# The third transform step one piece later, and the component sum of z ahead of its split

## The chip, the cores and the metric

One core of one Trainium2 chip runs the whole kernel. The time is that of the device for one execution, in microseconds; 2408.49 us is the median of three runs before the change (2408.03 to 2408.72). Shorter is better.

## The reference

For x of shape 2 x 1 x 4096 x 640 the kernel computes a gated mix of a spectral mixer a and a feed-forward block b:

```python
Xf = rfft2(x, axes=(1, 2))                    # 4096 tokens -> 2049 frequencies
zr, zi = Xf.real, Xf.imag                     # 4 blocks of 160 channels
hr = relu(zr @ w1[0] - zi @ w1[1] + b1[0])
hi = relu(zi @ w1[0] + zr @ w1[1] + b1[1])
or_ = hr @ w2[0] - hi @ w2[1] + b2[0]
oi_ = hi @ w2[0] + hr @ w2[1] + b2[1]
or_, oi_ = shrink(or_, 0.01), shrink(oi_, 0.01)
a = irfft2(or_ + 1j * oi_)
b = (gelu(x @ w_gate) * (x @ w_up)) @ w_down  # 640 -> 1728 -> 640
out = g * a + (1 - g) * b                     # g = sigmoid(sum(x * gate_w))
```

All values are 32-bit floats.

## The kernel before, in words

TensorE multiplies in a rounded format (float32r), so the kernel splits each operand into a high part (a rounded copy, helper `high`, L290, on ScalarE) and a low part (what the rounding left, helper `low`, L293, mostly a VectorE subtraction that reads the high part). A product is then the sum of two or three matmuls. PSUM has 8 banks, which `bank()` hands out in turn; each holds one result until the other engines have emptied it. The schedule is manual: each engine runs its instructions in the order in which the code issues them, and the waits between engines follow from which tiles and banks they share.

The work has three stages.

1. **Feed-forward up, with the first transform between its pieces** (to about 1278 us). There are 39 pieces: 3 groups of feature tiles x 13 pieces of tokens. The first piece runs `plain`, every other one `quad` for each of its four or five tiles; each quad has 7 places (`hook(0)` to `hook(6)`) where other work is issued. In pieces 14 to 24 and 26 to 36 these places also carry the first transform: 64 steps, one for each of two batches and 32 token residues. The list `steps_a` says which piece i, and which of its slots j, takes step k. A step loads x (`a_load`, SP's queue), splits it twice (`a_split`), computes a part of the gate (`a_gate`, L819) and runs two halves `a_step` (L832: two matmuls each, with L833 and L834 emptying the banks), and a store of the result (scr, SP's queue). Both halves multiply with tables `f`, one tile for each half with a single buffer; each set of tables serves four steps in a row, and `f1_load` (L797, on GpSimd's queue) fetches the next set behind the step k with k % 4 == 1.

2. **The spectral layers** (about 1278 to 1715 us). 16 chunks of frequencies x 4 blocks of channels are 64 steps. In step i the program issues: every fourth time, `rest` for the next chunk (a transform without sums, tile zz); `main_z` for step i + 1; `mlp1` for step i; `mlp2` for step i - 1; and every second step `y_split` and `inv1` for a pair of earlier blocks. `main_z` calls `fwd2`: eight matmuls (L1001) put the real and imaginary components of z side by side in one bank `pz`. The z copy (ScalarE, L290) and the z subtraction (VectorE, L293) split both components; the zt copy (ScalarE, L1013) takes the imaginary one and the addition (VectorE, L1016) makes zt = real + imaginary of it. `mlp1` multiplies the split zs of such a sum (tiles sh, sl) first, into a bank that ScalarE copies as kc (L1104); then VectorE forms hs from two more results and kc (L1111). Between the two, `sums()` splits zt of the next step into zs. ScalarE then rounds relu(hs) to h (L1064), VectorE subtracts (L1065), and a last bank is emptied by ScalarE (L1117) and VectorE (L1118). `mlp2` ends in m (L1148) and y (L1149). `y_split` makes ys; `inv1` ends in copies `is` on ScalarE (L1184) and VectorE (L1186).

3. **Inverse transform and feed-forward down** (from about 1715 us): 32 steps of `down`, which add both into the output.

The list and the four instructions that the change touches are

```python
    steps_a = [(i, j) for i in (*range(14, 25), *range(26, 37))
               for j in ((0, 1, 2) if i in (15, 17, 22) else (0, 1) if i < 26 or i == 36 else (3,) if i == 26 else (0, 1, 2, 3))]
```

and the body of `fwd2`, below with the functions that call it.

Of the kernel before, what the change touches and what calls it, by code (L numbers as in the profile page):

```python
# [234 lines left out]
def spectral_mix_kernel(ctx: ExitStack, tc: tile.TileContext, a):  # L235
    nc = tc.nc
# [11 lines left out]
    def bank():  # L248
        return psum.tile([P, 512], F32, name="bank", tag="bank")
# [39 lines left out]
    def high(dst, src, scale=1.0):  # L289
        nc.scalar.activation(dst, src, AF.Copy, scale=scale)  # L290

    def low(dst, src, hi, eng=nc.vector):
        eng.tensor_sub(dst, src, hi.bitcast(F32))  # L293

    def split(dst_h, dst_l, src, eng=nc.vector):

        high(dst_h, src)
        low(dst_l, src, dst_h, eng)
# [658 lines left out]
    def part_of(b, c, k):  # L957

        if not wide(b, c):
            return tiny([P, CH], name=("zt", "kc", "hs")[k])  # L960
        if not WT:
            WT.append(mid([P, 3, CW], name="wt"))
        return WT[0][:, k]
# [32 lines left out]
    def fwd2(b, c, o, z, zs=None):  # L996

        pz = bank()
        for kp in range(4):
            ft = F2[0 if c == 0 and kp == 0 else 1]  # L1000
            nc.tensor.matmul(pz.rearrange("p (r e k f) -> p k r e f", r=2, e=2, k=4)[:, kp], SC[b, c, kp][:, o:o + P],  # L1001
                             ft.rearrange("p (r e f) -> p r e f", r=2, e=2), start=True, stop=True)
        F = width(b, c)
        if F > CH:
            zz = [z[h][:, :, :F].rearrange("p r (e n) -> p r e n", e=2)[..., :P] for h in range(2)]
            pr = pz.rearrange("p (r e n) -> p r e n", r=2, e=2)
        else:
            zz, pr = [z[h][:, :, :F] for h in range(2)], pz.rearrange("p (r n) -> p r n", r=2)
        high(zz[0], pr)
        if zs:  # L1010
            t = part_of(b, c, 0)
            t4 = t[:, :F].rearrange("p (e n) -> p e n", e=2)[..., :P] if F > CH else t[:, :F]
            nc.scalar.activation(t4, pr[:, 1], AF.Copy)  # L1013
        low(zz[1], pr, zz[0])
        if zs:
            nc.vector.tensor_add(t4, pr[:, 0], t4)  # L1016
        if wide(b, c):
            pn = bank()
            for q in range(2):
                nc.tensor.matmul(pn[:, :4], SC[q, c, 0][:, o:o + P], fny[:, 4 * q:4 * q + 4], start=q == 0, stop=q == 1)  # L1020
            split(*(z[h][:, :, :F].rearrange("p r (e n) -> p r e n", e=2)[..., P] for h in range(2)),
                  pn[:, :4].rearrange("p (r f) -> p r f", r=2))
            if zs:
                nc.vector.tensor_copy(t[:, :F].rearrange("p (e n) -> p e n", e=2)[..., P], pn[:, :2])
        return lambda: split(zs[0][:, :F], zs[1][:, :F], t[:, :F])

    def rest(b, c):

        z = zmid(b, c, [P, 2, 2, width(b, c)], F32R, name="zz")
        fwd2(b, c, 4 * P, [z[:, h] for h in range(2)])  # L1030
        d = zld[b][c]
        if wide(b, c):
            st(d, z.rearrange("p h r f -> p (h r f)").bitcast(F32))
        else:
            st(dr(d, 0, [[4 * CW, P], [CW, 4], [1, CH]]), z[:, :, :, :CH].rearrange("p h r f -> p (h r) f").bitcast(F32))
# [12 lines left out]
    def main_z(b, c, n):  # L1048
        F = width(b, c)
        z = two(b, c, "z")  # L1050
        if wide(b, c):
            zs = small([P, 2, F], F32R, name="zs")
            zs = [zs[:, h] for h in range(2)]
        else:
            if chunks.index((b, c)) < 2 * NCH - 4:
                zs = mid([P, 2, F], F32R, name="zs")
                zs = [zs[:, h] for h in range(2)]
            else:
                zs = [tiny([P, F], F32R, name="zs") for h in range(2)]
        Z[b, c, n] = z, zs  # L1060
        return fwd2(b, c, P * n, z, zs)
# [472 lines left out]
    def spread(i, s, fs):  # L1534

        for k, f in enumerate(fs):
            j, q = i, max(s + k, 0)
            while j < last and q >= points(j):
                j, q = j + 1, q - points(j)
            slots.setdefault((j, q), []).append(f)  # L1540
    steps_a = [(i, j) for i in (*range(14, 25), *range(26, 37))
               for j in ((0, 1, 2) if i in (15, 17, 22) else (0, 1) if i < 26 or i == 36 else (3,) if i == 26 else (0, 1, 2, 3))]

    def back(i, s, f):
        if s < 0:
# [2 lines left out]
    for k, (b, n2) in enumerate(a_seq):  # L1548
        i, j = steps_a[k]
# [42 lines left out]
    for j in range(7):  # L1592
        p0, p1, p2 = wd_pre(j)
        i = 2 * KEYS
# [190 lines left out]
```

## Time and profile before

| what | value |
|---|---|
| median of three runs | 2408.49 us |
| the profiled execution | 2407.91 us, span 2406.1 us |
| granted TensorE clock | 1.000 |
| TensorE busy | 2397.7 us (100%) |
| VectorE busy | 1969.7 us (82%) |
| ScalarE busy | 1464.5 us (61%) |
| GpSimd busy | 143.0 us (6%) |
| DMA | 503.08 MB, mean 209 GB/s |

By stage, with the busy time of each engine (us):

| stretch | TensorE | VectorE | ScalarE |
|---|---|---|---|
| 0 to 1278 (1278) | 1275.20 | 992.34 | 752.94 |
| 1278 to 1715 (437) | 436.45 | 374.24 | 346.46 |
| 1715 to 2406 (691) | 686.01 | 603.15 | 365.14 |

In rows of the profile PE is TensorE, PEld its loading of weights, DVE VectorE, ACT ScalarE, POOL GpSimd and SP the engine that issues most DMAs. In rows in order of time the columns are start (us from the start of the span), duration (us), engine, line, operation, result<-operands, shapes and number; brackets hold how long the engine was idle just before, and what ended that. In rows of waits the numbers are us in total, how many times, and the longest. In rows by stretch each engine has its busy time and its number of instructions, in the order PE, PEld, DVE, ACT, POOL; then come the granted clock, the DMA share and GB/s.

### The profile page before, as it was taken

What the parts mean: (1) busy time and instruction counts of PE and PEld (TensorE: products, weight loads), DVE (VectorE), ACT (ScalarE), POOL (GpSimd) and SP (SyncE); (2) the same over time, 40 slices, a digit from 0 to 9 for tenths busy, and PEclk for the clock granted to TensorE, in tenths of its full rate; (3) what the DMA queues carried; (4) which work ended last, traced back from release to release, by engine and by line L of the source; (5) the groups of instructions that cost most, each with busy time, mean ns of one, the idle gap of its engine ahead of it and who ended that gap; (6) DMA issues with size and microseconds to landing.
All of it is one profiled execution on the core that took longest, in us unless ns stands there. A gap on an engine that the chain in (4) does not pass through costs nothing.

```text
span 2406.1 us, 49143 instructions
## 1 busy us (share of the span) xinstructions
PE 2397.7 (100%) x18047; PEld 2391.9 (99%) x18047; DVE 1969.7 (82%) x4150; ACT 1464.5 (61%) x3332; POOL 143.0 (6%) x213
## 2 busy tenths in 40 slices
PE   9999999999999999999999999999999999999999
PEld 9999999999999999999999999999999999999999
DVE  8777779777778888888857888888898888888887
ACT  5544456665566666666645788888755555555554
POOL 0111110000000000000001111111000000000000
PEclk9999999999999999999999999999999999999999
DMA  5666666777776777868766454557955544455543
GB/s 213 246 232 235 229 229 231 257 257 252 254 258 228 242 262 239 287 228 268 250 207 230 130 169 152 163 167 234 339 163 165 165 151 152 145 164 165 163 147 98
DMA packets 319093, 503.08 MB, mean 209 GB/s; under 512 B 24444, under 2 KB 196348, under 8 KB 318852
## 3 DMA queue, kind: packets, MB, share of 16 engines
q1 hardware_dynamic: 298788, 446.65, 55.5%
q0 software_dynamic: 20064, 53.29, 6.2%
q8 instruction: 142, 2.33, 0.4%
q14 instruction: 99, 0.81, 0.1%
HBM read 308.74 MB, written 191.11 MB: 208 GB/s over the span
## 4 chain that ended last, share of the span: by engine, by line
PE 91%; issue 5%; DVE 2%; DMA 1%; ACT 1%; SPq 0%; POOL 0%; POOLq 0%; DVEq 0%; ACTq 0%
PE bank L578 70%; PE bank L312 13%; PE bank L1001 3%; PE bank L709 2%; PE bank L832 1%; DMA f<-in_f_dram 1%; PE bank L1087 1%; PE bank L1088 1%; DMA xraw<-in_xT_dram 0%; DVE w L293 0%; PE bank L1089 0%; DVE xo L293 0%; DVE hs L1111 0%; DVE xd L489 0%; ACT m L1148 0%
## 5 line engine op out<-in xcount | busy, mean ns | idle before, releaser
L578 PE MATMUL bank<-xo,w 128*128 128x320 f32 (+1 forms) x9000 | 1250.4, 297 | 0.7 <-ACT p L605 0.7
L578 PEld LDWEIGHTS bank<-xo,w 128*128 128x128 f32 x9000 | 1220.0, 189 | 1.8 <-ACT p L605 1.1
L578 PE MATMUL bank<-wx,ho 128*128 128x320 f32 x4608 | 631.8, 299 | 1.3 <-DVE ho L293 1.1
L578 PEld LDWEIGHTS bank<-wx,ho 128*128 128x128 f32 x4608 | 627.7, 189 | 1.8 <-DVE ho L293 1.4
L293 DVE TENSOR_TENSOR ho<-hraw,ho 128x640 fp32r<-128x640 f32 (+3 forms) x384 | 194.1, 539 | 24.7 <-ACT ho L290 22.7
L605 ACT ACTIVATE u<-bank 128x320 f32<-128x320 f32 (+1 forms) x250 | 107.4, 430 | 138.1 <-PE bank L578 134.2
L290 ACT ACTIVATE ho<-hraw 128x640 fp32r<-128x640 f32 x320 | 168.9, 571 | 34.5 <-PE bank L578 31.3
L655 DVE TENSOR_TENSOR u<-bank,u 128x320 f32<-128x320 f32 (+1 forms) x165 | 79.9, 485 | 82.7 <-ACT u L605 81.8
L293 DVE TENSOR_TENSOR xs<-xr,xs 64x640 fp32r<-64x640 f32 x128 | 104.9, 820 | 46.6 <-ACT xs L290 43.3
L834 DVE TENSOR_TENSOR as<-bank,as 64x320 f32<-64x320 f32 x256 | 113.8, 483 | 25.9 <-ACT as L833 24.1
L293 DVE TENSOR_TENSOR xo<-xraw,xo 128x640 fp32r<-128x640 f32 (+1 forms) x155 | 125.0, 806 | 8.1 <-ACT xo L290 6.1
L312 PE MATMUL bank<-wm,h 128*128 128x320 f32 (+1 forms) x792 | 129.3, 299 | 0.0
L605 ACT ACTIVATE p<-bank 128x320 f32<-128x320 f32 (+1 forms) x125 | 54.1, 432 | 119.3 <-PE bank L578 61.9
L833 ACT ACTIVATE as<-bank 64x320 f32<-64x320 f32 x256 | 96.6, 426 | 32.3 <-PE bank L832 29.3
L290 ACT ACTIVATE xo<-xraw 128x640 fp32r<-128x640 f32 (+1 forms) x155 | 111.7, 721 | 5.4 <-DMA xraw<-in_xT_dram 3.6
L1405 ACT ACTIVATE bank<-bank 128x320 f32<-128x320 f32 x31 | 13.1, 422 | 166.4 <-PE bank L578 166.4
L312 PEld LDWEIGHTS bank<-wm,h 128*128 128x128 f32 (+1 forms) x792 | 111.8, 186 | 1.1
L1399 DVE SCALAR_TENSOR_TENSOR uu<-bank,gs,uu 128x320 f32<-128x320 f32 x193 | 102.5, 545 | 8.4 <-PE bank L578 4.9
L1371 DVE SCALAR_TENSOR_TENSOR uu<-bank,gs,uu 128x320 f32<-128x320 f32 x120 | 57.9, 545 | 49.2 <-ACT uu L1370 47.1
L290 ACT ACTIVATE xs<-xr 64x640 fp32r<-64x640 f32 x128 | 93.4, 730 | 2.1 <-DMA xr<-in_x_dram 0.3
L606 ACT ACTIVATE h<-bank 128x320 f32<-128x320 f32 (+1 forms) x165 | 71.1, 431 | 35.8 <-PE bank L578 32.8
L605 ACT ACTIVATE pb<-bank 128x320 f32<-128x320 f32 x80 | 35.0, 437 | 88.8 <-PE bank L578 88.6
(184 smaller groups left out, 3520.7 us busy)
## 6 DMA issues: line engine op xcount, KB each, us to landing
xo<-xD SPq DMA_DIRECT2D x96, 640.0 KB
xraw<-in_xT_dram SPq DMA_DIRECT2D x158, 320.0 KB
hD<-h SPq DMA_DIRECT2D x128, 320.0 KB
hraw<-hD SPq DMA_DIRECT2D x128, 320.0 KB
xD<-xo POOLq DMA_DIRECT2D x48, 640.0 KB, 4.4
sc<-scr SPq DMA_DIRECT2D x65, 320.0 KB
xr<-in_x_dram SPq DMA_DIRECT2D x64, 320.0 KB
scr<-as SPq DMA_DIRECT2D x64, 320.0 KB
```

What stands on the lines that cost most here:

```text
L290: nc.scalar.activation(dst, src, AF.Copy, scale=scale)
L293: eng.tensor_sub(dst, src, hi.bitcast(F32))
L312: nc.tensor.matmul(dst, l, by_two(r), start=i == 0, stop=i == len(ops) - 1)
L578: nc.tensor.matmul(dst, l, by_two(r), start=first and i == 0, stop=i == len(ops) - 1, skip_group_check=True)
L605: copy = lambda d, s_: nc.scalar.activation(d, s_, AF.Copy)
L606: gelu = lambda d, s_: nc.scalar.activation(d, s_, AF.Gelu_apprx_tanh)
L655: nc.vector.tensor_add(u4, C, u4)
L833: nc.scalar.activation(stg[hi, cs], pa[lo, :320], AF.Copy)
L834: nc.vector.tensor_add(stg[hi, cs], pa[hi, :320], stg[hi, cs])
L1001: nc.tensor.matmul(pz.rearrange("p (r e k f) -> p k r e f", r=2, e=2, k=4)[:, kp], SC[b, c, kp][:, o:o + P], ft.rearrange("p (r e f) -> p ...
L1371: nc.vector.scalar_tensor_tensor(uu[n2][:, cs], po[:, :320], gs[b][:, k, n2:n2 + 1], uu[n2][:, cs], op0=OP.mult, op1=OP.add)
L1399: nc.vector.scalar_tensor_tensor(dst, x, g, dst, op0=OP.mult, op1=OP.add)
```

## The change

```diff
@@ fwd2 @@
-        high(zz[0], pr)
         if zs:
             t = part_of(b, c, 0)
             t4 = t[:, :F].rearrange("p (e n) -> p e n", e=2)[..., :P] if F > CH else t[:, :F]
             nc.scalar.activation(t4, pr[:, 1], AF.Copy)
+            nc.vector.tensor_add(t4, pr[:, 0], t4)
+        high(zz[0], pr)
         low(zz[1], pr, zz[0])
-        if zs:
-            nc.vector.tensor_add(t4, pr[:, 0], t4)
...
@@ steps_a @@
-               for j in ((0, 1, 2) if i in (15, 17, 22) else (0, 1) if i < 26 or i == 36 else (3,) if i == 26 else (0, 1, 2, 3))]
+               for j in ((0, 1, 2) if i in (15, 18, 22) else (0, 1) if i < 26 or i == 36 else (3,) if i == 26 else (0, 1, 2, 3))]
```

No instruction is added, removed or resized. The second hunk takes the third slot from piece 17 and gives piece 18 one. So step 9 goes from slot 2 of piece 17 to slot 0 of piece 18, step 10 from slot 0 to slot 1 of piece 18, and step 11 from slot 1 to slot 2; all other steps stay. Step 9 is one behind which the next set of tables is loaded.

TensorE, in the first quad of piece 18 (the rows show the first transform's matmuls, L832, which read a table f1, between those of the quad). Before:

```order
L578 MATMUL bank_6594<-xo_6298,w3_4960 128x320 x3
L578 MATMUL bank_6594<-xo_6298,w3_4961 128x320 x3
L832 MATMUL bank_6774<-xs_6731,f1_6686 128x320
L832 MATMUL bank_6778<-xs_6731,f1_6686 128x320
L578 MATMUL bank_6629<-xo_6256,w1_4946 128x320 x6
```

Now:

```order
L578 MATMUL bank_6586<-xo_6298,w3_4960 128x320 x3
L578 MATMUL bank_6586<-xo_6298,w3_4961 128x320 x3
L832 MATMUL bank_6744<-xs_6701,f1_6017 128x320
L832 MATMUL bank_6748<-xs_6701,f1_6017 128x320
L578 MATMUL bank_6620<-xo_6256,w1_4946 128x320 x6
```

f1_6686 is the third set's first half, loaded just before; f1_6017 is the second set's, which three earlier steps have used already. The third set (f1_6760 now) is first read at the next slot, in the fourth quad of the piece.

ScalarE, in a spectral step (z_18147 is the high part of z, zt the sum, kc, zs and h as above; the brackets name the engine or DMA queue whose semaphore an instruction waits for). Before:

```order
L1184 ACTIVATE is_18127<-bank_18128 128x320 [waits DMAHW6_49,PE_49,Activation_49]
L290 ACTIVATE z_18147<-bank_18149 128x512 [waits PE_49]
L1013 ACTIVATE zt_18155<-bank_18149 128x256
L1104 ACTIVATE kc_18164<-bank_18160 128x256 [waits PE_49]
L290 ACTIVATE zs_18148<-zt_18155 128x256 [waits DVE_49]
L1064 ACTIVATE h_18159<-hs_18165 128x512 [waits DVE_49]
```

Now:

```order
L1183 ACTIVATE is_18127<-bank_18128 128x320 [waits DMAHW6_49,PE_49,Activation_49]
L1012 ACTIVATE zt_18154<-bank_18149 128x256 [waits PE_49]
L290 ACTIVATE z_18147<-bank_18149 128x512 [waits DVE_49]
L1103 ACTIVATE kc_18164<-bank_18160 128x256 [waits PE_49]
L290 ACTIVATE zs_18148<-zt_18154 128x256
L1063 ACTIVATE h_18159<-hs_18165 128x512 [waits DVE_49]
```

The zt copy has moved ahead of the z copy; the z copy now waits for VectorE, and the copy to zs no longer does.

VectorE, in the same step. Before:

```order
L1186 COPY is_18127<-bank_18133 128x320 [waits PE_49]
L293 TENSOR_TENSOR z_18147<-bank_18149,z_18147 128x512 [waits PE_49,Activation_49]
L1016 TENSOR_TENSOR zt_18155<-bank_18149,zt_18155 128x256
L1111 TENSOR_TENSOR hs_18165<-bank_18167,kc_18164 128x256 [waits PE_49,Activation_49]
L1111 TENSOR_TENSOR hs_18165<-bank_18167,kc_18164 128x256
```

Now:

```order
L1185 COPY is_18127<-bank_18133 128x320 [waits PE_49]
L1013 TENSOR_TENSOR zt_18154<-bank_18149,zt_18154 128x256 [waits Activation_49]
L293 TENSOR_TENSOR z_18147<-bank_18149,z_18147 128x512 [waits Activation_49]
L1110 TENSOR_TENSOR hs_18165<-bank_18167,kc_18164 128x256 [waits PE_49,Activation_49]
L1110 TENSOR_TENSOR hs_18165<-bank_18167,kc_18164 128x256
```

The addition stands ahead of the subtraction, and each of the two has a wait for ScalarE of its own; before, the one wait of the subtraction served both. Lines behind `fwd2` count one less in the changed kernel.

## The prediction

> **What bounds the kernel now.** I read the page first, then the waits of TensorE, then the waits of the spectral stretch, and last the order of time on three engines inside single steps of it.
>
> ```profile
> PE 2397.7 (100%) x18047; PEld 2391.9 (99%) x18047; DVE 1969.7 (82%) x4150; ACT 1464.5 (61%) x3332; POOL 143.0 (6%) x213
> ```
>
> TensorE is busy for 2397.7 of 2406.1 us, so the kernel can gain 8 us at most without less arithmetic. It can lose more: the other engines only have to make TensorE wait. Its waits that touch the two edits are small:
>
> ```profile
> PE bank L832 <- DMA f<-in_f_dram: 0.9, 1, 0.9
> ...
> PE bank L312 <- DVE hs L1118: 0.5, 2, 0.3
> ```
>
> The first is one wait of the first transform for its weights, the second a pair of waits in the spectral layers. That the spectral layers wait so little does not mean that they have room. These are the waits from 1381 to 1715 us:
>
> ```profile
> ACT zs L290 <- DVE zt L1016: 45.6, 54, 1.0
> ...
> ACT h L1064 <- DVE hs L1111: 12.5, 54, 0.3
> ...
> DVE zz L293 <- ACT zz L290: 3.4, 12, 0.3
> ```
>
> ScalarE waits twice for VectorE in each of 54 steps. Those are links of a ring: h of one step (L1064) to h of the next. I measured the ring from the starts of L1064. Here are four successive ones, with some of what stands between them on ScalarE:
>
> ```profile
> 1399.55 0.63 ACT L1064 ACTIVATE h<-hs 128x512 fp32r<-128x512 f32 x1 [0.24 <-DVE hs L1111]
> ...
> 1403.79 0.58 ACT L290 ACTIVATE z<-bank 128x512 fp32r<-128x512 f32 x1
> ...
> 1406.39 0.63 ACT L1064 ACTIVATE h<-hs 128x512 fp32r<-128x512 f32 x1 [0.25 <-DVE hs L1111]
> ...
> 1409.53 0.59 ACT L290 ACTIVATE z<-bank 128x512 fp32r<-128x512 f32 x1
> 1410.01 0.38 ACT L1013 ACTIVATE zt<-bank 128x256 f32<-128x256 f32 x1
> ...
> 1411.47 0.42 ACT L290 ACTIVATE zs<-zt 128x256 fp32r<-128x256 f32 x1 [0.82 <-DVE zt L1016]
> 1412.14 0.63 ACT L1064 ACTIVATE h<-hs 128x512 fp32r<-128x512 f32 x1 [0.24 <-DVE hs L1111]
> ...
> 1415.90 0.59 ACT L290 ACTIVATE z<-bank 128x512 fp32r<-128x512 f32 x1
> 1416.38 0.38 ACT L1013 ACTIVATE zt<-bank 128x256 f32<-128x256 f32 x1
> ...
> 1418.50 0.63 ACT L1064 ACTIVATE h<-hs 128x512 fp32r<-128x512 f32 x1 [0.18 <-DVE hs L1111]
> ```
>
> The intervals are 6.84, 5.75 and 6.36 us. Call them C (a step that also splits zz), B (one that also copies is) and A (neither); A and C also split ys. The first and the last interval of the regular stretch begin and end here:
>
> ```profile
> 1381.65 0.63 ACT L1064 ACTIVATE h<-hs 128x512 fp32r<-128x512 f32 x1 [0.24 <-DVE hs L1111]
> ```
>
> ```profile
> 1708.67 0.63 ACT L1064 ACTIVATE h<-hs 128x512 fp32r<-128x512 f32 x1 [0.24 <-DVE hs L1111]
> ```
>
> The 54 waits of L1064 give 53 intervals over 327.02 us, B in every second place: 27 B, 12 C (the 12 waits of zz) and 14 A. 27 x 5.75 + 14 x 6.36 + 12 x 6.84 = 326.4 us. So all but 0.6 us of this stretch goes at the ring's own pace, and the ring has no slack against TensorE:
>
> ```profile
> 1382.92 0.47 DVE L1118 SCALAR_TENSOR_TENSOR hs<-bank,b1r,hs 64x256 f32<-64x256 f32 x1
> ```
>
> ```profile
> 1383.45 0.60 PE L312 MATMUL bank<-zs,wm 128*128 128x256 f32 x3 [0.29 <-DVE hs L1118]
> ```
>
> L1118 empties a PSUM bank at 1383.39 and the matmul that takes the bank starts 0.06 us later. Ring and TensorE go side by side, one touching the other. A longer ring lengthens the kernel; a shorter one finds TensorE in the way at once:
>
> ```profile
> 1381.65:1406.34 24.69, 24.35 (x197) 23.97 (x196) 21.43 (x48) 20.22 (x49) 3.13 (x2) 1.00 0.52 160
> ```
>
> This is one chunk of four steps (2B + A + C): 24.69 us, TensorE busy 24.35.
>
> **Edit 1, the third step one piece later.** The step that reads the third set of weights:
>
> ```profile
> 522.93 0.43 PE L832 MATMUL bank<-xs,f 128*128 128x320 f32 x2
> 529.71 0.51 PE L832 MATMUL bank<-xs,f 128*128 128x320 f32 x2 [0.90 <-DMA f<-in_f_dram]
> 533.59 0.43 PE L832 MATMUL bank<-xs,f 128*128 128x320 f32 x2
> 547.44 0.43 PE L832 MATMUL bank<-xs,f 128*128 128x320 f32 x2
> ```
>
> ```profile
> 522.31 0.53 POOL L797 DMA_DIRECT2D f<-in_f_dram  x1 [49.19 <-PE bank L832]
> ```
>
> Each half of the weights has one buffer, so its load is issued only when the last step with the old half is done: here at 522.31, for use some 7 us later, too late by 0.90. With the step in piece 18, old weights serve where 529.71 and 533.59 stand, and the new ones are first read near 547.44: about 18 us from load to use for a transfer that took 7. The wait goes; with the restart of TensorE I take **-1.0 us** (0.9 to 1.1). What else moves with the step: its x load and scr store on SP, two splits, the gate and the evictions. Nothing waits for these two DMAs but the step itself, and pieces 15 and 22 hold a third step already without a row of theirs among TensorE's waits. I cost them at nothing, covered by TensorE's matmuls; if a bank came late there, it would be a part of a microsecond once.
>
> **Edit 2, the addition ahead of the split.** Nothing is added or removed; 64 steps issue the same four instructions on one bank in another order. Before: two copies on ScalarE (z, zt), then a subtraction and the addition on VectorE, one crossing. Now: ScalarE zt, VectorE addition, ScalarE z, VectorE subtraction, three crossings. The rows of the order in the section on the change show that the z copy, which waited for TensorE before, now waits for VectorE. That this is the addition, and not some older work, follows from how such a bank is handled before:
>
> ```profile
> 1415.41 0.82 DVE L293 TENSOR_TENSOR ys<-y,ys 128x640 fp32r<-128x640 f32 x1 [0.20 <-ACT ys L290]
> 1416.79 0.69 DVE L293 TENSOR_TENSOR z<-bank,z 128x512 fp32r<-128x512 f32 x1 [0.55 <-PE bank L312]
> 1417.40 0.41 DVE L1016 TENSOR_TENSOR zt<-bank,zt 128x256 f32<-128x256 f32 x1
> 1417.73 0.74 DVE L1111 TENSOR_TENSOR hs<-bank,kc 128x256 f32<-128x256 f32 x2
> ```
>
> The subtraction needs only the z copy, which ended at 1416.49, and VectorE was free from 1416.23. It started at 1416.79, 0.03 us after the end of the zt copy (1416.76), which only reads the same bank. So on one bank VectorE stands behind everything ScalarE was given ahead of it, and the reverse must hold for the z copy behind the addition. The Trainium skill bears on this (PSUM — Partial Sum Buffer, section on PSUM bank collisions): two engines on one bank at once raise an error, reads against reads too, so programs guard a bank with semaphores. By that rule the wait has to be there and the sum is that of the forecast; by data alone it would be the first rival. The 0.03 us agree with the rule.
>
> Now each interval again, with 0.03 us for a crossing (as above), and with the habit of these rows that an instruction that waits for nothing starts 0.08 us before the end of the one ahead of it on VectorE:
>
> A: zt copy first, 1415.90 + 0.38 = 1416.28; addition 1416.31 to 1416.72; z copy 1416.75 to 1417.34; subtraction 1417.37; 0.61 later (as now) hs at 1417.98 against 1417.73: **+0.25**.
>
> ```profile
> 1409.43 0.89 DVE L1186 COPY is<-bank 128x320 f32<-128x320 f32 x2
> 1410.42 0.69 DVE L293 TENSOR_TENSOR z<-bank,z 128x512 fp32r<-128x512 f32 x1
> 1411.03 0.41 DVE L1016 TENSOR_TENSOR zt<-bank,zt 128x256 f32<-128x256 f32 x1
> 1411.36 0.74 DVE L1111 TENSOR_TENSOR hs<-bank,kc 128x256 f32<-128x256 f32 x2
> ```
>
> B: the zt copy would end at 1409.91, but VectorE copies until 1410.32. Addition 1410.24 to 1410.65; z copy 1410.68 to 1411.27; subtraction 1411.30; hs 1411.91 against 1411.36: **+0.55**. VectorE now stands idle for 0.6 us while ScalarE does what it formerly did during the copies.
>
> ```profile
> 1403.92 0.69 DVE L293 TENSOR_TENSOR zz<-bank,zz 128x512 fp32r<-128x512 f32 x1 [0.28 <-ACT zz L290]
> ...
> 1405.61 0.74 DVE L1111 TENSOR_TENSOR hs<-bank,kc 128x256 f32<-128x256 f32 x2
> ```
>
> C: the zt copy would end by 1404.2, but VectorE is at zz until 1404.61. Addition 1404.53 to 1404.94; z copy (0.58) 1404.97 to 1405.55; subtraction 1405.58; hs 1406.19 against 1405.61: **+0.58**.
>
> ScalarE's wait of 0.82 before zs goes, since zt is summed earlier; but zs was never on the ring, for h waits for hs. Behind hs all is as before: h, L1118, the next step. The kc copy stands behind the z copy and still ends before hs wants it. Sum: 27 x 0.55 + 14 x 0.25 + 12 x 0.58 = **+25.3 us**. The 0.6 us in which the ring waited for others is absorbed.
>
> The nine intervals ahead of 1381.65 (the first chunk and the wide one) have the same edit, but there the ring waits for TensorE:
>
> ```profile
> 1374.15 0.52 ACT L1148 ACTIVATE m<-bank,neg2lam 2x320 f32<-2x320 f32 x1 [0.56 <-PE bank L312]
> ```
>
> Between 0 (all hidden) and 9 x 0.58 = 5.2 I take 1.5, nearer to nothing because of this wait.
>
> Sum: -1.0 + 25.3 - 0.6 + 1.5 = +25.2 us. The profiled execution took 2407.91 us (span 2406.1), 0.6 under the median 2408.49 of the runs. 2407.9 + 25.2 = **2433.1 us**.
>
> Bounds of the unseen crossing: if VectorE were always ready in time, each interval would cost A's 0.25, 53 x 0.25 = 13.3, with nothing for the first nine: 2419.6. If VectorE were always late, the addition (0.41 less 0.08), z copy and crossings stand in full between its work: 0.41 + 0.03 + 0.59 + 0.03 + 0.61 against 0.61 + 0.33 is +0.73 each, 53 x 0.73 = 38.7, and 5.2 for the nine: 2450.
>
> **Rivals.** (1) The z copy doesn't wait, and only data count: the change then does what it seems to do. In A the subtraction could start 0.03 after the z copy, at 1416.78 with the addition already done, and hs comes 0.34 earlier, in B 0.18, in C 0.14. TensorE (24.35 of 24.69) lets at most 0.3 us of each chunk's 0.84 through: 13 x 0.3 + 1.0 = -4.9, 2403 us. It decides as soon as the z copy starts before the addition ends. Against it stand the 0.03 us above. 4 in 100. (2) The delay is hidden in ScalarE's 0.82: only edit 1 counts, 2407. Against it: that wait ends with the same addition whose delay is in question. 5 in 100. (3) VectorE's copies come early enough everywhere, 2419 to 2422: 9 in 100. (4) The longer ring catches on something further, a bank of fwd2 held until the later subtraction, towards 2450: 9 in 100.
>
> **How the numbers follow.** The forecast has 73 in 100, with 2426 to 2440 as its own range. 2421 to 2442 takes in most of rivals 3 and leaves out about 2 in 10. A measurement can tell about 0.2%, 4.8 us: faster by more, 3 in 100 (rival 1 at its full size); within it, 6 (the rest of 1, and 2); slower by more, 91.
>
> **What would show it.** In the changed profile: no wait of L832 for f; a VectorE wait for ScalarE of about 0.65 us before each subtraction in the spectral steps; ScalarE waiting for the addition before the z copy instead of before zs; L1064 every 6.3 (B), 6.6 (A) and 7.4 us (C); TensorE waiting about 1 us for L1118 in every second step, some 25 us in all. I am wrong if L1064 keeps its 5.75, 6.36 and 6.84, or if TensorE's waits lie elsewhere.

## The result, and the profile after

| | before | changed |
|---|---|---|
| median (us) | 2408.6 of 4 runs | 2436.86 of 4 runs (2436.59 to 2437.68) |
| ratio | | 1.0118, 95% interval 1.0101 to 1.0136 |
| the profiled execution (us) | 2407.91, span 2406.1 | 2436.59, span 2434.8 |
| granted TensorE clock | 1.000 | 1.000 |

The changed kernel is slower by about 28 us. Among the kernels below, one of the four executions of the one with the sum ahead in odd blocks took 5124.02 us instead of 2422.80 to 2423.37, at the same clock of 1.000; why is not known, and it moves that kernel's median by 0.2 us. Line numbers behind `fwd2` are one less than before: h is L1063, its subtraction L1064, kc L1103, hs L1110 and L1117; inside it the zt copy is L1012 and the addition L1013.

The busy row of the changed kernel's page:

```profile
PE 2409.7 (99%) x18047; PEld 2394.6 (98%) x18047; DVE 1972.7 (81%) x4150; ACT 1464.8 (60%) x3332; POOL 142.9 (6%) x213
```

No engine has an instruction more than before, and VectorE and ScalarE are busy for as long as before within 3 us. So the 28 us are waiting, not work. TensorE's 12 us of additional "busy" are no work either, with the same 18047 matmuls: the records of matmuls in a row overlap (before, eight of L1001, 0.28 us each, fill 1.05 us together), and where the next one starts later they overlap less. Here are TensorE's longest waits in the changed kernel (us in total, times, longest):

```profile
PE bank L312 <- DVE hs L1117: 16.3, 27, 0.7
PE bank L1502 <- DVE zero L1498: 1.2, 1, 1.2
...
PE bank L578 <- DMA wx<-wdf: 0.5, 1, 0.5
```

The row for f is gone (edit 1). The row for the last hs, 0.5 us in two waits before, has become 16.3 us in 27: one in every second spectral step. The same stretch of 53 ring intervals, first before, then changed (busy time and instructions of PE, PEld, DVE, ACT, POOL; clock, DMA share, GB/s):

```profile
1381.65:1708.67 327.02, 326.48 (x2645) 324.94 (x2644) 284.63 (x624) 267.31 (x649) 40.15 (x27) 1.00 0.60 188
```

```profile
1383.12:1737.04 353.92, 337.39 (x2644) 328.11 (x2643) 287.30 (x624) 267.63 (x649) 39.97 (x27) 1.00 0.56 174
```

26.90 of the 28.7 us between the two spans arise here, with the same instructions on every engine but for one matmul and one load at the edge of the stretch. These are the waits in it (1381 to 1741 us) that belong to the ring:

```profile
ACT h L1063 <- DVE hs L1110: 45.8, 54, 0.9
ACT z L290 <- DVE zt L1013: 39.5, 54, 1.1
DVE z L293 <- ACT z L290: 35.9, 54, 0.7
...
PEld bank L312 <- DVE hs L1117: 21.4, 27, 0.9
```

The second and third row are new, and stand in each of 54 steps: ScalarE's z copy waits for the addition, then VectorE's subtraction waits 0.66 us for the z copy. ScalarE's wait for hs grew from 12.5 to 45.8 us, and its wait for the sum ahead of zs is gone. One interval in order of time, of kind B, first on ScalarE (the last three rows give the lengths of a C, a B and an A):

```profile
1425.36 0.74 ACT L1183 ACTIVATE is<-bank 128x320 f32<-128x320 f32 x2
1425.99 0.37 ACT L1012 ACTIVATE zt<-bank 128x256 f32<-128x256 f32 x1
1427.15 0.60 ACT L290 ACTIVATE z<-bank 128x512 fp32r<-128x512 f32 x1 [0.79 <-DVE zt L1013]
1427.64 0.38 ACT L1103 ACTIVATE kc<-bank 128x256 f32<-128x256 f32 x1
1427.91 0.42 ACT L290 ACTIVATE zs<-zt 128x256 fp32r<-128x256 f32 x1
1429.17 0.63 ACT L1063 ACTIVATE h<-hs 128x512 fp32r<-128x512 f32 x1 [0.84 <-DVE hs L1110]
...
1436.62 0.63 ACT L1063 ACTIVATE h<-hs 128x512 fp32r<-128x512 f32 x1 [0.84 <-DVE hs L1110]
...
1442.93 0.63 ACT L1063 ACTIVATE h<-hs 128x512 fp32r<-128x512 f32 x1 [0.84 <-DVE hs L1110]
...
1449.57 0.63 ACT L1063 ACTIVATE h<-hs 128x512 fp32r<-128x512 f32 x1 [0.84 <-DVE hs L1110]
```

and on VectorE:

```profile
1425.90 0.89 DVE L1185 COPY is<-bank 128x320 f32<-128x320 f32 x2
1426.70 0.42 DVE L1013 TENSOR_TENSOR zt<-bank,zt 128x256 f32<-128x256 f32 x1
1427.78 0.69 DVE L293 TENSOR_TENSOR z<-bank,z 128x512 fp32r<-128x512 f32 x1 [0.66 <-ACT z L290]
1428.39 0.75 DVE L1110 TENSOR_TENSOR hs<-bank,kc 128x256 f32<-128x256 f32 x2
```

The zt copy ends at 1426.36, but VectorE is at its is copies until 1426.79. The addition ends at 1427.12, the z copy runs from 1427.15 to 1427.75, the subtraction starts at 1427.78, hs at 1428.39. Before, the z copy ran beside VectorE's copies; now it runs while VectorE waits. The intervals are 7.45 (C), 6.31 (B) and 6.64 us (A), where they were 6.84, 5.75 and 6.36.

Edit 1 shows on TensorE, in piece 18 of the changed kernel:

```profile
528.39 0.43 PE L832 MATMUL bank<-xs,f 128*128 128x320 f32 x2
532.19 0.43 PE L832 MATMUL bank<-xs,f 128*128 128x320 f32 x2
546.05 0.43 PE L832 MATMUL bank<-xs,f 128*128 128x320 f32 x2
```

and on GpSimd's queue, where the load of the next tables is issued:

```profile
529.12 0.53 POOL L797 DMA_DIRECT2D f<-in_f_dram  x1 [55.71 <-PE bank L832]
```

The load is issued at 529.12 and its tables are first read at 546.05, 16.9 us later, without a wait.

### The profile page after: what moved, and what is told of

Same layout as the page of the kernel before. It is cut to its first block, busy times and chain, and to the rows that moved or that the text cites. A ratio compares the mean times of both kernels' runs of the same rounds, so it can differ in the third digit from the quotient of the medians.

```text
span 2434.8 us, 49196 instructions
## 1 busy us (share of the span) xinstructions
PE 2409.7 (99%) x18047; PEld 2394.6 (98%) x18047; DVE 1972.7 (81%) x4150; ACT 1464.8 (60%) x3332; POOL 142.9 (6%) x213
## 4 chain that ended last, share of the span: by engine, by line
PE 88%; DVE 6%; ACT 4%; DMA 2%; issue 1%; SPq 0%; ACTq 0%; DVEq 0%
PE bank L578 74%; PE bank L312 8%; PE bank L709 2%; PE bank L832 1%; DVE hs L1110 1%; PE bank L1001 1%; ACT h L1063 1%; DVE h L1064 1%; ACT kc L1103 1%; DVE y L1148 0%; DVE is L1185 0%; DVE hs L1117 0%; ACT zs L290 0%; DMA wx<-wdf 0%; DMA wraw<-in_wgu_dram 0%
```

## The experiments

Times are medians beside runs of the kernel before on the same chip, whose own medians were 2408.0 to 2408.6. B, A and C are the length that most intervals of the kind have. "Ring" is the length of the 53 intervals, from the start of one h to that of the 53rd after it.

| kernel | time (us) | ratio and 95% interval | B | A | C | ring |
|---|---|---|---|---|---|---|
| before | 2408.6 | 1 | 5.75 | 6.36 | 6.84 | 327.02 |
| the change | 2436.86 | 1.0118 (1.0101 to 1.0136) | 6.32 | 6.64 | 7.45 | 353.92 |
| third step alone | 2407.44 | 0.9997 (0.9987 to 1.0006) | 5.75 | 6.36 | 6.85 | 327.22 |
| sum ahead alone | 2437.37 | 1.0121 (1.0106 to 1.0136) | 6.32 | 6.64 | 7.45 | 354.01 |
| both copies first | 2407.49 | 0.9996 (0.9986 to 1.0006) | 5.75 | 6.36 | 6.84 | 327.17 |
| sum off the bank | 2413.62 | 1.0023 (1.0013 to 1.0032) | 5.56 | 7.09 | 7.09 | 333.72 |
| sum ahead in odd blocks | 2423.17 | 1.0063 (1.0046 to 1.008) | 6.32 | 6.36 | 6.84 | 342.24 |
| sum ahead in even blocks | 2420.46 | 1.0053 (1.0038 to 1.0068) | 5.75 | 6.70 | 7.45 | 338.94 |
| subtraction of z behind hs, old order | 2402.72 | 0.9977 (0.9968 to 0.9987) | 5.56 to 5.98 | 6.22 | 6.70 | 322.79 |
| doubling off the bank | 2407.47 | 1.0000 (0.999 to 1.0009) | 5.42 | 6.95 | 6.96 | 327.72 |
| subtraction of z behind hs, new order | 2423.92 | 1.0066 (1.0049 to 1.0083) | 6.13 | 6.35 | 7.22 | 342.02 |
| whole split of z behind hs, new order | 2402.91 | 0.9979 (0.997 to 0.9989) | 5.90 to 5.98 | 5.88 | 6.69 | 322.75 |

### One half of the change at a time

Edit 1 alone, in the kernel before:

```diff
-               for j in ((0, 1, 2) if i in (15, 17, 22) else ...
+               for j in ((0, 1, 2) if i in (15, 18, 22) else ...
```

> The third step one piece later, alone. Theory: TensorE's one wait of 0.9 us for the weights f goes, nothing else changes, and L1064 keeps its intervals of 5.75, 6.36 and 6.84 us; 2407.2 to 2407.9 us where the kernel before takes 2408.6. Rival (the moved step adds waits of its own in piece 18, and part of the 28 us of the change is made there): over 2410 us, with TensorE waiting between 525 and 560 us.

The time is 0.9 us under that of the runs beside it, which its interval cannot tell from nothing; the trace can, for TensorE's waits have no row for f any more. These are the longest of them in this kernel:

```profile
PE bank L1503 <- DVE zero L1499: 1.2, 1, 1.2
PE bank L578 <- DVE ho L293: 1.1, 1, 1.1
PE bank L578 <- ACT p L605: 0.7, 1, 0.7
```

Edit 2 alone is the hunk of `fwd2`, with the list of steps as before:

```diff
+            nc.vector.tensor_add(t4, pr[:, 0], t4)
+        high(zz[0], pr)
         low(zz[1], pr, zz[0])
-        if zs:
-            nc.vector.tensor_add(t4, pr[:, 0], t4)
```

> The addition ahead of the split, alone. Theory: all of the loss is here; 2437.0 to 2438.0 us (the change's 2436.9 plus the 0.7 us of the wait for f, which is there again), L1063 every 6.32, 6.64 and 7.45 us in the regular stretch. Rival (both edits carry part of the loss): under 2434 us.

It has the whole loss: all intervals are those of the changed kernel. The gain of 0.9 and the loss of 29.0 us, each alone, add up to the 28.3 of both together, so the two edits do not touch each other.

### Is it VectorE's order, or the z copy between two of its instructions?

Both copies run on ScalarE before VectorE starts on the bank, and VectorE still adds first and subtracts second:

```diff
             nc.scalar.activation(t4, pr[:, 1], AF.Copy)
-            nc.vector.tensor_add(t4, pr[:, 0], t4)
         high(zz[0], pr)
+        if zs:
+            nc.vector.tensor_add(t4, pr[:, 0], t4)
         low(zz[1], pr, zz[0])
```

> As the change, but ScalarE makes the zt copy and the z copy both before VectorE's addition and subtraction, so that the bank passes from ScalarE to VectorE once and not back; VectorE still has the addition ahead of the subtraction. Theory (the loss is the two extra crossings of the bank): the ring is as long as before, intervals of 5.75, 6.36 and 6.84 us within 0.05, time 2407 to 2409 us. Rival (the loss comes of VectorE's own order: the subtraction and with it the bank come free later): intervals of 6.3, 6.6 and 7.4 us again and 2432 to 2437 us.

The ring is back at its pace of before. So the order of VectorE's two instructions costs nothing here; what costs is that the z copy stands between them.

### Does the z copy wait because of the bank?

The addition no longer reads the bank:

```diff
-            nc.vector.tensor_add(t4, pr[:, 0], t4)
+            nc.vector.tensor_add(t4, t4, t4)
```

> As the change, but the addition adds the zt copy to itself instead of the real component out of the bank (so zt is not the sum; this part of the computation is left out). It stands at the same place, needs the same zt copy, and no longer touches the bank. Theory (the z copy waits for the addition only because both are on one bank): the z copy doesn't wait for VectorE, and the subtraction waits for the z copy alone; the ring is then shorter than before by 0.34 in A, 0.18 in B and 0.14 us in C, TensorE becomes the bound and lets a part of it through: 2402 to 2406 us. Rival (the place of the addition itself costs the time, by whatever it delays): 2432 to 2437 us.

B fell as expected, but A and C grew, and the time was 8 us above the range. In the B steps the z copy starts before the addition does, as these rows of ScalarE and VectorE in this kernel show:

```profile
1409.18 0.37 ACT L1012 ACTIVATE zt<-bank 128x256 f32<-128x256 f32 x1
1409.45 0.59 ACT L290 ACTIVATE z<-bank 128x512 fp32r<-128x512 f32 x1
```

```profile
1409.89 0.42 DVE L1013 TENSOR_TENSOR zt<-zt 128x256 f32<-128x256 f32 x1
...
1415.77 1.62 DVE L1013 TENSOR_TENSOR zt<-zt 128x256 f32<-128x256 f32 x1
```

With no bank in common there is no wait, and B is 0.18 shorter than before the change, which is what rival 1 had worked out for a z copy that doesn't wait. The second row of VectorE shows what took the gain in A and C: the same addition takes 1.62 us instead of 0.42. GpSimd at that time:

```profile
1415.55 1.56 POOL L293 TENSOR_TENSOR ys<-y,ys 128x640 fp32r<-128x640 f32 x1 [11.08 <-DMA zl<-zl]
```

GpSimd works until 1417.11, and the addition ends 0.28 later, at 1417.39. Of 28 additions that overlapped such work of GpSimd, 27 took 0.80 to 1.66 us and ended 0.28 after it; the 36 others took 0.42 at most. The 28th began 0.12 us ahead of GpSimd, and there GpSimd took longer, 1.72 us where its 28 other subtractions of ys took 1.54 to 1.57:

```profile
1441.08 0.43 DVE L1013 TENSOR_TENSOR zt<-zt 128x256 f32<-128x256 f32 x1
```

```profile
1441.20 1.72 POOL L293 TENSOR_TENSOR ys<-y,ys 128x640 fp32r<-128x640 f32 x1 [11.44 <-DMA zl<-zl]
```

That interval, an A, took 6.04 us, 0.32 less than before, where rival 1 had 0.34. All operands of this addition lie in SBUF. That of the changed kernel, with one operand in PSUM, overlapped GpSimd's work 28 times as well and took 0.41 to 0.43. The Trainium skill (SBUF — State Buffer, section "SBUF: two separate sides") has VectorE and GpSimd share a pair of ports, and names VectorE instructions with two inputs in SBUF among those that can't run beside one of GpSimd that reads SBUF; these rows agree. To see whether one operand in SBUF escapes it:

```diff
-            nc.vector.tensor_add(t4, pr[:, 0], t4)
+            nc.vector.tensor_scalar(t4, t4, 2.0, None, op0=OP.mult)
```

> As the sum off the bank, but VectorE doubles the zt copy (one operand, so zt is again not the sum) instead of adding two operands from SBUF. In the run with the addition off the bank, B took 5.56 us as expected, but in A and C the addition took up to 1.6 us while GpSimd subtracted for ys. Theory (that was the two SBUF operands beside GpSimd; without them the ring is shorter than before in every step): 2402 to 2405 us, A and C not above 6.4 and 6.9 us. Rival (any VectorE instruction at that place is held up beside GpSimd): again about 2413 us.

It does not: the range was missed by 2.5 us, and the instruction is held too. All of the kernel's L1013 in a view by line (shortest, median and longest in ns):

```profile
L1013 DVE TENSOR_SCALAR zt<-zt x60: 281/285/1535, 1306.5 to 1706.5; 128x256 f32<-128x256 f32 x60
```

So two operands in SBUF can't be the only reason. Nor did it take the 2413 us of the rival: the instruction itself is 0.13 us shorter than the addition (0.285 against 0.42), and so is each kind of interval, by 0.13 to 0.14. The same section of the Trainium skill names a second kind, a VectorE mode that uses both ports; whether this instruction ran in one, no run here shows. For the question of this section both kernels answer alike: B falls to 5.56 and 5.42 once the bank isn't shared, and what A and C show is another effect. Both kernels take away the bank and one operand together, so they show the wait's place and price, not a rule of PSUM: the program sets that wait as a semaphore.

### Do the kinds of interval pay what was worked out for each?

The addition goes ahead only in odd blocks (their steps are the B), then only in even ones (A and C), with `== 0` in the first line:

```diff
+        first = zs and o // P % 2 == 1
+        if first:
             nc.vector.tensor_add(t4, pr[:, 0], t4)
         high(zz[0], pr)
         low(zz[1], pr, zz[0])
+        if zs and not first:
+            nc.vector.tensor_add(t4, pr[:, 0], t4)
```

> As the change, but the addition stands ahead of the split only for odd channel blocks, whose four instructions fall into the B intervals; for even blocks it stands behind the subtraction. Theory (each step pays for its own extra crossings, +0.57 in B): 27 x 0.57 = 15.4 us and at most 1.5 us ahead of the regular stretch, over 2407.4 of the third step alone: 2422 to 2424.5 us; B intervals of 6.32, A and C at 6.36 and 6.84 us. Rival (a loss by the step, the same in each): half of the 29.5 us, 2422, but then the even blocks alone give 2422 too. Rival (the loss comes from a chain over several steps, so that half of the steps hide it): under 2415 us.

> The other half: addition ahead only for even blocks (A and C intervals). Theory: 14 x 0.27 + 12 x 0.61 = 11.1 us and up to 2 us ahead of the regular stretch, over 2407.4: 2418.5 to 2421 us; A 6.64, C 7.45, B at 5.75 us. Rival (a loss by the step, the same in each): 2422 us. Rival (a chain over several steps): under 2415 us.

Both times lie in their ranges, and each kind pays alone nearly what it pays in the change: the ring grows by 15.2 us with the odd blocks and by 11.9 with the even ones, together 27.1 against 26.9 for the whole. Only A, expected at 6.64, stands mostly at 6.70 when it pays alone; why, no run here shows. So there is hardly any slack that one kind of step could lend to the other.

### Off the ring

The subtraction that the crossing delays is not needed for hs. In this kernel (edit 1 with it) ScalarE has its old order, VectorE adds first, and the subtraction stands in `sums()`, which is issued behind hs:

```diff
-        low(zz[1], pr, zz[0])
         if zs:
             nc.vector.tensor_add(t4, pr[:, 0], t4)
+        else:
+            low(zz[1], pr, zz[0])
...
-        return lambda: split(zs[0][:, :F], zs[1][:, :F], t[:, :F])
+        def sums():
+            low(zz[1], pr, zz[0])
+            split(zs[0][:, :F], zs[1][:, :F], t[:, :F])
+        return sums
```

> The third step one piece later, and ScalarE's order of before (z copy, zt copy); on VectorE the addition comes first and the subtraction of z goes behind hs, with the split of zs. The bank passes from ScalarE to VectorE once and is held longer than in any other version. Theory (the ring from h to h is the bound; 0.61 us of VectorE's work leave it in each step, and TensorE becomes the bound): chunks of 24.4 to 24.5 us instead of 24.69, no wait of TensorE for the bank of L1118; 2403 to 2405.5 us, the fastest of all. Rival (what costs is that the bank of fwd2 is emptied late): slower than 2408 us. Rival (the ring was never the bound): 2407.4 us.

It is faster than both kernels, a little more than expected. One chunk of it as a stretch:

```profile
1400.00:1424.46 24.46, 24.46 (x203) 24.46 (x202) 21.42 (x48) 20.76 (x50) 3.14 (x2) 1.00 0.56 162
```

TensorE is busy for all of it, and its waits have no row for hs any more. That points to TensorE as what now sets the pace, at 24.46 us a chunk against 24.69 before; the last kernel of this section bears it out.

The changed kernel with the same move of the subtraction alone, the z copy staying behind the addition:

```diff
         high(zz[0], pr)
-        low(zz[1], pr, zz[0])
+        if not zs:
+            low(zz[1], pr, zz[0])
```

> The whole change, with the subtraction of z behind hs; the z copy still waits for the addition. Theory (the ring goes on over whatever is late for hs; now that is kc, which ScalarE copies behind the z copy): hs 0.21 us later than before in B, 0.08 earlier in A, 0.26 later in C; +0.60 in a chunk of 24.69, 13 chunks, +7.8 over 2407.4: 2413 to 2417 us, hs waiting for kc. Rival (the loss lies in the late subtraction alone): TensorE's bound, 2402 to 2404 us. Rival (any crossing of the bank costs what it cost in the change): over 2430 us.

The wait moved to hs, which now waits for the kc copy behind the late z copy, as expected; the size was missed by 7 us. ScalarE's h at the end of a B interval, and VectorE around it:

```profile
1439.35 0.63 ACT L1068 ACTIVATE h<-hs 128x512 fp32r<-128x512 f32 x1 [0.52 <-DVE hs L1115]
```

```profile
1438.56 0.76 DVE L1115 TENSOR_TENSOR hs<-bank,kc 128x256 f32<-128x256 f32 x2 [0.94 <-ACT kc L1108]
1439.23 0.68 DVE L293 TENSOR_TENSOR z<-bank,z 128x512 fp32r<-128x512 f32 x1
1439.83 0.42 DVE L293 TENSOR_TENSOR zs<-zt,zs 128x256 fp32r<-128x256 f32 x1
1440.16 0.69 DVE L1069 SCALAR_TENSOR_TENSOR h<-hs,h 128x512 fp32r<-128x512 f32 x1
```

I had left out that the moved subtraction now stands ahead of that of h, which I take to be on the ring too: h starts at 1439.35, and its subtraction 0.81 later instead of 0.66 to 0.67. That is 0.15 us for most intervals, while B, A and C came 0.17, 0.07 and 0.12 longer than worked out. So it fits the miss as a whole but not kind by kind, and no run takes this cause alone.

TensorE's waits have just one row for the last hs (L1122) in this kernel too, a single wait of 0.2 us, although it takes 16 us longer than the kernel without the change. One stretch of it:

```profile
1383.00:1712.00 329.00, 326.29 (x2554) 316.57 (x2554) 270.50 (x600) 259.32 (x626) 39.42 (x26) 1.00 0.57 176
```

So neither waits that are nearly gone nor a TensorE that is busy for 99% of a stretch show that TensorE sets the pace.

Last, z copy and subtraction both behind hs, in the changed kernel:

```diff
-        high(zz[0], pr)
-        low(zz[1], pr, zz[0])
+        if not zs:
+            split(zz[0], zz[1], pr)
...
         def sums():
+            split(zz[0], zz[1], pr)
             split(zs[0][:, :F], zs[1][:, :F], t[:, :F])
```

> The whole change, with both the z copy and the subtraction behind hs, so kc no longer stands behind the z copy. The bank still passes three times between ScalarE and VectorE, but the two later passes are off the ring. Theory: TensorE is the bound as in the run with the split behind hs; 2402 to 2404 us. Rival (three crossings cost wherever they stand): over 2410 us.

ScalarE and VectorE still cross three times on the bank, in the order of the change, and nothing is lost. VectorE in this kernel:

```profile
1426.39 0.41 DVE L1013 TENSOR_TENSOR zt<-bank,zt 128x256 f32<-128x256 f32 x1
1426.72 0.75 DVE L1114 TENSOR_TENSOR hs<-bank,kc 128x256 f32<-128x256 f32 x2
1427.47 0.69 DVE L293 TENSOR_TENSOR z<-bank,z 128x512 fp32r<-128x512 f32 x1
```

and the z copy on ScalarE:

```profile
1426.84 0.60 ACT L290 ACTIVATE z<-bank 128x512 fp32r<-128x512 f32 x1 [0.56 <-DVE zt L1013]
```

hs follows the addition at once, and the z copy runs beside hs. The ring takes 322.75 us here and 322.79 in the first kernel of this section, with different orders on ScalarE and VectorE, and TensorE is busy for all of it in both: there it does set the pace.

## Why the prediction was right

The forecast was 2433.1 us; the kernel took 2436.86. Point by point, by spans:

| term (us) | predicted | measured |
|---|---|---|
| edit 1, start of the span to the first h | -1.0 | -0.74 |
| first nine intervals | +1.5 | +2.21 |
| 53 intervals, with the 0.6 taken as absorbed | +24.7 | +26.90 |
| behind the last h | 0 | +0.32 |
| sum | +25.2 | +28.7 |

Of the 3.5 us that the sum was short, 2.2 lie in the 53 intervals and 0.7 in the first nine.

**What bounds the kernel.** Right. The ring and TensorE ran side by side: each interval that grew showed in full (odd and even blocks apart), and where the ring shrank TensorE was in the way after 0.23 us a chunk. A busy share of 100% on TensorE before the change did not mean that the other engines had room.

**Edit 1.** Right in mechanism; the wait for f is gone, in the change and alone. About 0.3 us of the gain is not in the span up to the first h. It is within what that stretch varies between executions, since the same edit alone gave -0.67 and the second edit alone +0.87.

**Edit 2, the mechanism.** Right: the z copy waits for the addition in all 54 steps, and starts 0.03 us after its end (0.09 in two of them). Both copies ahead of the addition bring the old pace back, and with the addition off the bank the z copy goes ahead of it. With the rule of the Trainium skill that the prediction weighed (PSUM — Partial Sum Buffer, on PSUM bank collisions) the trace agrees as far as ScalarE and VectorE are never on that bank at once in these rows; that an overlap would raise an error, no run here shows.

**Edit 2, the sizes.** B, A and C were forecast as 6.30, 6.61 and 7.42 and came as 6.32, 6.64 and 7.45. The 0.02 to 0.03 are a z copy of 0.60 instead of 0.58 to 0.59 us and rounding; over 53 intervals they make 1.1 us. Two smaller steps failed:

- The 0.6 us by which the ring fell behind its own pace were not absorbed. Nearly all irregular intervals grew like the others (an A from 6.43 to 6.69, a C from 6.90 to 7.51), so these delays lie on the ring, not beside it.
- One A, the last, grew by 0.75 instead of 0.25. There VectorE makes both subtractions of ys. Its rows in the kernel before, where the subtraction of z follows without a wait, and in the changed kernel:

```profile
1701.16 0.69 DVE L293 TENSOR_TENSOR z<-bank,z 128x512 fp32r<-128x512 f32 x1
```

```profile
1726.72 1.56 DVE L293 TENSOR_TENSOR ys<-y,ys 128x640 fp32r<-128x640 f32 x2 [0.18 <-ACT ys L290]
1728.20 0.42 DVE L1013 TENSOR_TENSOR zt<-bank,zt 128x256 f32<-128x256 f32 x1
```

The zt copy had ended at 1727.59, so the addition came 0.6 us late. VectorE was the late one both before and after, which is the case that the prediction priced at 0.73 for its upper bound; this interval should have had that price.

**The first nine intervals.** The term was chosen between nothing and 5.2, without a sum of its own, and came at 2.21, 0.7 above it.

**The rivals.** Rival 1 fell with the z copy's wait, but its prices held where a run could show them: off the bank, B was 0.18 shorter, and the one A without a hold by GpSimd 0.32. Rival 2 fell, as ScalarE's wait for the sum vanished and the ring still grew. Rival 3 needed VectorE on time in B and C, where it stayed at its copies and at zz until after the zt copy. Rival 4, a further catch, left no term of its size: the pieces above add up to the 28.7.

**The signs named.** All were there, but TensorE's waits for L1117 came to 16.3 us, not 25: the rest of the 26.9 stands in its busy time (337.39 us against 326.48), as the section on the result has it.

## What to carry to other kernels

Where two engines hand work to each other once in every step, measure the time from one such instruction to the next: if it repeats to 0.01 us, something sets that pace, however little the engines wait. What sets it is not told by the repeat, by rows of waits or by TensorE's busy share (in the first kernel off the ring, where TensorE is the bound, the intervals repeat as well, at 5.98, 6.22, 5.56 and 6.70), but by kernels that make the chain longer and shorter. Before two instructions change places, ask what the second engine does meanwhile: here the two additional handovers, at 0.03 us each, are worth 0.06 us by themselves, but they drew 0.6 us of a copy, which had run beside other work, between two instructions of the ring. And a result that the next link doesn't need belongs behind that link: with the split of z behind hs even the new order ran 5 us faster than the kernel before.

## What was not expected of the hardware

A VectorE instruction whose operands all lie in SBUF was held while GpSimd worked on one that it had begun earlier: 0.42 us became up to 1.66 for the addition, 0.285 up to 1.54 for the doubling. The one time that the addition began first, GpSimd's instruction was the longer one, by 0.16 us. The hold shows as a longer instruction, not as a wait, and so in no row of waits. With an operand in PSUM the addition was not held, in 28 overlaps of 28.
